# Decode attention with a gated feed-forward on one core: maxima over partitions on GpSimd, w1 and w3 multiplied on VectorE, two programs moved to block boundaries

## The chip, the cores and the metric

The kernel runs on one core of a Trainium2 chip. The metric is the device time of one execution in microseconds; lower is better. All data are float32.

## What is computed

One token x (512 values) goes through grouped-query attention over a cache of 32768 positions (32 query heads, 8 key and value heads, 128 values a head) and through a gated feed-forward (1792 hidden values); a sigmoid gate mixes the two.

```python
def _A_ref(x, k_cache, v_cache, wq, wo):
    q = (x @ wq).reshape(B, Sq, Hq, Dh).transpose(0, 2, 1, 3)
    k = jnp.repeat(k_cache, rep, axis=1)
    v = jnp.repeat(v_cache, rep, axis=1)
    scores = jnp.einsum("bhqd,bhkd->bhqk", q, k) * (Dh ** -0.5)
    p = softmax(scores, axis=-1)
    o = jnp.einsum("bhqk,bhkd->bhqd", p, v)
    return o.transpose(0, 2, 1, 3).reshape(B, Sq, Hq * Dh) @ wo

def _B_ref(x, w1, w3, w2):
    return (silu(x @ w1) * (x @ w3)) @ w2

g = sigmoid((x * gate_w).sum(-1, keepdims=True))
out = g * _A_ref(...) + (1 - g) * _B_ref(...)
```

The caches are 134 MB each and the weights 28 MB in all; every byte is read once.

## The kernel before, in words

**Buffers and loads.** Two large buffers in SBUF, big_a and big_b, have two halves each; the names A0, A1, B0, B1 stand for the halves. All loads go through SyncE's queue in the order of the source: `load` (issued at line 191) and `load_credit` (line 413, values). An issue waits until the readers of its half are done, and everything behind it in the queue waits too. The order is wq (A0, A1), w1 (B0), w3 (B1), then tiles of 4 MB of keys into one half each, then keys and values by turns.

**Start.** GpSimd fills the constants (lines 215 to 225): `ident` with a select at line 218, `ones`, and zeros for padding. Line 255 turns x into columns `xp`. Line 270 multiplies wq. In the block `ff` (line 307) TensorE multiplies w1 and w3 by x, 16 products of 448 columns for each matrix, into the PSUM banks `pf[2]` and `pf[3]`. Lines 313 to 320 make the gated hidden row and turn it.

**Loop.** There are 16 key tiles `t` (4 groups `w` of 4). For each half of a tile VectorE transposes the keys in four parts of 2048 columns (line 355, `kt`), and TensorE multiplies them with a window of the queries (line 344). After both halves ScalarE copies the scores out (line 361). After each fourth tile TensorE turns the scores (`turn`, line 371) into `turned`, four PSUM banks. TensorE's part is a loop in its program (lines from 658 on); the other engines' parts are written out. The values follow the keys by four tiles: `softmax(w)` runs once for each group, behind the key transposes of a tile on VectorE; `weights` (line 418) and `values_all` (line 430) then multiply a tile of values in big_b, and only after that SyncE may load the next values there.

**Softmax.** Line 381 takes the maximum over the free dimension into `mt` (128 x 8). The maximum over the partitions is taken on VectorE: a transpose of 32 x 32 blocks (383), four reductions (385) and one over their results (387), four copies that spread it (390), a transpose back (392). The result `top` is subtracted in place (393), ScalarE takes the exponentials (398), VectorE their sums (403). The queue of VectorE is in order.

**End.** The last group's softmax stands outside the loop, behind `own(11)`. It is followed by the division (`norm`), the placing of heads, and the products with wo (`mix`, line 527), each of which frees `wo_t` for the next load of wo. The last values, wo and w2 arrive while those run; lines 617 to 641 are the last products, the copy of the result, and its write, for which GpSimd waits at the very end.

Of the kernel before, what the change touches and what calls it, by code (L numbers as in the profile page):

```python
# [1 line left out]

# [7 lines left out]
ALU = mybir.AluOpType  # L10
AX = mybir.AxisListType
PE = mybir.EngineType.PE

P = 128
# [102 lines left out]
def kernel(  # L117
# [16 lines left out]
    F = w1.shape[1]  # L134
    HQ = wq.shape[1] // DH
    REP = HQ // HKV
    NC = D // P
# [12 lines left out]
    FJ = F // 4  # L150
# [17 lines left out]
    win = sbuf("win", NP, 4, 48)  # L168
    winc = sbuf("winc", 4, 32)
    probs = sbuf("probs", 2, 65 * 16)  # L170
    prob = [probs[:, u, :] for u in range(2)]
    pv = sbuf("pv", 33 * 16)
# [5 lines left out]
    otp = sbuf("otp", 8, 32)  # L178
    htp = sbuf("htp", FR, 32)
    turned = nc.alloc_psum_tensor("turned", [P, 2048], F32)[:]  # L180
    pf = [turned[:, 512 * f:512 * f + 512] for f in range(4)]
# [12 lines left out]
    def region(b, z):  # L194
        return big[b][:, z * R:(z + 1) * R]

    wqd = wq.rearrange("(p c) n -> p (c n)", c=NC)
    for z in range(2):
        load(region(0, z), wqd[:, z * R:(z + 1) * R], [f"A{z}"])
        if z == 0:  # L200
            load(rows[0][0:1, :], x.rearrange("a b n -> (a b) n"), ["row0"])
            pr.add("ACT", lambda: nc.scalar.dma_start(rows[1][0:1, :], gate_w.rearrange("(o n) -> o n", o=1)),
                   writes=["row1"], inc="gate", by=16)
# [1 line left out]
        load(region(1, z)[:, 0:NC * F], t.rearrange("(p c) f -> p (c f)", c=NC), [f"B{z}"])  # L205


    ident, ones, fold = sbuf("ident", P), sbuf("ones", P), sbuf("fold", 32)
    own_b, own_q, own_k, own_x = sbuf("own_b", 4), sbuf("own_q", 4), sbuf("own_k", 8), sbuf("own_x", 16)
    spot, mask, xp = sbuf("spot", 8, 16), sbuf("mask", 8), sbuf("xp", NC, 32)  # L210
    gate, sums, recip, on = sbuf("gate", 2), sbuf("sums", 32), sbuf("recip", 32), sbuf("on", 32)
    mt, mtt = sbuf("mt", 32), sbuf("mtt", 32)
    quads, high, wide_t, top = sbuf("quads", 4), sbuf("high", 1), sbuf("wide_t", 32), sbuf("top", 32)
    G = nc.gpsimd
    pool(lambda: G.memset(acc, 0.0), writes=["acc"])
    pool(lambda: G.memset(xp, 0.0), writes=["xp0"])
# [2 lines left out]
        out=ident, in_=ident, compare_op=ALU.not_equal, fill=1.0, base=0, pattern=[[-1, P]], channel_multiplier=1,  # L219
    ), reads=["ident0"], writes=["ident"])  # L220
    pool(lambda: G.memset(ones, 1.0), writes=["ones"])
    for n, t in (
        ("win0", win), ("otp", otp), ("mt", mt), ("pvpad", pv[:, 512:528]), ("pad0", prob[0][:, 1024:1040]), ("pad1", prob[1][:, 1024:1040])
    ):
        pool(lambda t=t: G.memset(t, 0.0), writes=[n])

    for src, dst, view, axes in (
# [11 lines left out]
            reads=[src], writes=[dst])  # L239
# [24 lines left out]
    for c in range(NC):  # L264
# [19 lines left out]
        reads=["gate0"], writes=["gate1"])  # L284
# [4 lines left out]
    for b in range(2):  # L289
        qt = kt[b][:, 0:512]  # L290
        dve(lambda b=b, qt=qt: V.transpose(qt, rows[b]), reads=[f"row{b}"], writes=[f"kt{b}"])
        for j in range(4):
            w, u = divmod(4 * b + j, 2)
            src = qt[32 * j:32 * j + 32, :].rearrange("p (q c x) -> p x c q", q=4, c=4)[:, 0]
            for e in range(2):
                r, o = 2 * u + e, 16 + 8 * e + 4 * u
                dst = win[32 * r:32 * r + 32, w, :, o:o + 4]
                act(lambda d=dst, s=src: A.copy(d, s), reads=[f"kt{b}", "win0"], writes=[("win", w, r)])


    for z in range(2):
        def ff(z=z):
            t = region(1, z)
            for c in range(NC):
                for j in range(4):
                    o = c * F + FJ * j
                    ins = T.matmul(  # L307
                        pf[2 + z][32 * j:32 * j + 32, 0:FJ], xp[:, c, :], t[:, o:o + FJ],
                        start=(c == 0), stop=(c == NC - 1),
                    )  # L310
            return ins
        pe(ff, reads=[f"B{z}", "xp"], writes=[f"f{2 + z}"])
    act(lambda: A.activation(silu[:, 0:FJ], pf[2][:, 0:FJ], AF.Sigmoid), reads=["f2"], writes=["silu0"])
    dve(lambda: V.tensor_mul(silu[:, 0:FJ], silu[:, 0:FJ], pf[2][:, 0:FJ]), reads=["f2", "silu0"], writes=["tmp0"])

# [62 lines left out]
    def softmax(w):  # L378
        banks = [f"f{f}" for f in range(4)]

        dve(lambda: V.tensor_reduce(mt[:, 0:8], turned.rearrange("p (n q) -> p q n", q=8), axis=AX.X, op=ALU.max),  # L381
            reads=banks, writes=["mt"])
        dve(lambda: V.transpose(mtt, mt), reads=["mt"], writes=["mtt"])
        for k in range(4):
            dve(lambda k=k: V.tensor_reduce(quads[0:32, k:k + 1], mtt[32 * k:32 * k + 32, :], axis=AX.X, op=ALU.max),  # L385
                reads=["mtt"], writes=[("quads", k)])
        dve(lambda: V.tensor_reduce(high[0:32, :], quads[0:32, :], axis=AX.X, op=ALU.max),
            reads=[("quads", k) for k in range(4)], writes=["high"])
        for k in range(4):
            dve(lambda k=k: V.tensor_copy(wide_t[32 * k:32 * k + 32, :], high[0:32, :].to_broadcast([32, 32])),  # L390
                reads=["high"], writes=[("wide_t", k)])
        dve(lambda: V.transpose(top, wide_t), reads=[("wide_t", k) for k in range(4)], writes=["top"])
        dve(lambda: V.tensor_tensor(  # L393
            turned.rearrange("p (n q) -> p n q", q=8), turned.rearrange("p (n q) -> p n q", q=8),
            top[:, 0:8].unsqueeze(1).to_broadcast([P, 256, 8]), op=ALU.subtract,
        ), reads=["top"], writes=banks)
        for u in range(2):
            act(lambda u=u: A.activation(  # L398
                prob[u][:, 0:1024].rearrange("p (y n q) -> p n y q", y=16, q=4),
                turned.rearrange("p (n y u q) -> p n y u q", n=16, y=16, u=2)[:, :, :, u],  # L400
                AF.Exp, scale=SCALE,
            ), reads=banks, writes=[("prob", u)])
        dve(lambda: V.tensor_reduce(  # L403
            sums[:, 8 * w:8 * w + 8].rearrange("p (u q) -> p u q", u=2),
            probs[:, :, 0:1024].rearrange("p u (n q) -> p u q n", q=4), axis=AX.X, op=ALU.add,
        ), reads=[("prob", u) for u in range(2)], writes=[("sums", w)])
# [46 lines left out]
    for t in range(NH):  # L453
        v = t - LAG
        scores(t, 0, first)
        second = window(t, 1)
        if v >= 1:
            own(v - 1)
            if v % 4:
                vals[v] = (vals[v], weights(v))  # L460
        scores(t, 1, second)
        scores_out(t)
        if t + 1 < NH:
            load_keys(t + 1)
            first = window(t + 1, 0)

        if v >= 0 and v % 4 == 0:
            softmax(v // 4)
            vals[v] = (vals[v], weights(v))
        if v >= 0:  # L470
            values_loop(*vals.pop(v))
        if v + 1 >= 0 and t + 1 < NH:
            vals[v + 1] = load_values(v + 1)
        if t % 4 == 3:
            turn()
# [89 lines left out]
    load(big[1], vd[6, 1], ["B0", "B1"])  # L565
    own(11)
    softmax(3)
    norm(range(4))
    heads(range(6))
# [65 lines left out]
    for a, b in parts[2:]:  # L635
        ff_down([(htp[:, k, :], w2t[:, k, :], k == 8, k == FR - 1) for k in range(a, b)], reads=["htp", ("w2", a)])
        if a == 8:
# [4 lines left out]
           reads=["res"], inc="out", by=16)  # L642


    for e in ("SP", "ACT", "DVE", "POOL"):
        pr.emit(e)
    ops = pr.ops["PE"]
# [60 lines left out]
```

## Time and profile before

| what | value |
|---|---|
| median of three runs | 696.18 us (696.12 to 696.57) |
| the profiled execution's own time | 695.86 us |
| its span in the profile | 694.0 us |
| busy: PE, DVE, ACT, POOL | 402.1, 376.2, 45.3, 2.6 us |
| bytes read from HBM | 296.23 MB |

The profile is one execution. The own time is what the clock of the device gave for it; the span runs from the first to the last instruction that was recorded, so about 1.9 us lie around it. PE is TensorE, DVE VectorE, ACT ScalarE, POOL GpSimd, SP SyncE; a q behind the name means the engine's sequencer, which issues DMAs. In the timeline a row has its start, its duration, engine, line, operation, output and input, and in brackets how long the engine was idle before and what released it.

### The profile page before, as it was taken

The numbers are of one execution on the slowest core, as the hardware profiler recorded it, in microseconds if no ns is written. First come the engines' busy times: TensorE is split into PE (matmuls) and PEld (weight loads), VectorE is DVE, ScalarE is ACT, GpSimd is POOL, SyncE is SP. The second block draws the span as 40 slices with busy tenths as digits, with TensorE's granted clock in tenths as the row PEclk, the third lists the DMA queues.
The fourth block names the chain that finished last, engine by engine and source line by source line (L and its number), as shares of the span: only waits on it lengthen the run. The fifth ranks groups of instructions, "written<-read, shape, count | busy, mean of one in ns | idle before, by whom it ended". The sixth has DMA issues, their size and how long they took to land. (4 is left out here: it accounts for less than half of the span.)

```text
span 694.0 us, 5676 instructions
## 1 busy us (share of the span) xinstructions
PE 402.1 (58%) x2400; PEld 92.6 (13%) x2400; DVE 376.2 (54%) x263; ACT 45.3 (7%) x90; POOL 2.6 (0%) x15
## 2 busy tenths in 40 slices
PE   3636566647556554746667644538456555376756
PEld 1100001101010110201010101201010101131112
DVE  1029999885719081686619091786529090654121
ACT  0200000020100000010100000020100000100000
POOL 1000000000000000000000000000000000000000
PEclk9966877877887796867665898977876776777679
DMA  9999999999999999999999999999999999999996
GB/s 391 421 425 444 431 425 433 467 399 427 451 419 431 444 448 404 450 423 427 465 406 448 416 442 419 442 431 450 427 423 434 419 472 399 447 425 424 427 422 285
DMA packets 9380, 296.34 MB, mean 427 GB/s; under 512 B 1046, under 2 KB 1050, under 8 KB 1436
## 3 DMA queue, kind: packets, MB, share of 16 engines
q1 hardware_dynamic: 9362, 296.23, 99.2%
q8 instruction: 5, 0.08, 0.0%
q14 instruction: 3, 0.02, 0.0%
q10 hardware_dynamic: 10, 0.00, 0.0%
HBM read 296.23 MB, written 0.00 MB: 427 GB/s over the span
## 5 line engine op out<-in xcount | busy, mean ns | idle before, releaser
L355 DVE STREAM_TRANSPOSE kt<-big_a 128x2048 f32<-128x2048 f32 x112 | 250.2, 2287 | 182.3 <-DMA big_a<-in_A_k_cache_dram 180.8
L344 PE MATMUL ps<-kt,winc 128*32 128x512 f32 x1024 | 186.1, 807 | 132.7 <-PEq L658 132.7
L430 PE MATMUL ps<-big_b,pv 128*32 128x512 f32 x768 | 110.2, 738 | 74.0 <-PEq L658 74.0
L344 PEld LDWEIGHTS ps<-kt,winc 128*32 128x32 f32 x1024 | 26.5, 122 | 287.0 <-issue 287.0
L430 PEld LDWEIGHTS ps<-big_b,pv 128*32 128x32 f32 x768 | 30.3, 132 | 153.7 <-issue 153.7
L355 DVE STREAM_TRANSPOSE kt<-big_b 128x2048 f32<-128x2048 f32 x16 | 35.7, 2287 | 3.2 <-DMA big_b<-in_A_k_cache_dram 3.2
L527 DVE SCALAR_TENSOR_TENSOR acc<-wo_t,own_rows,acc 128x512 f32<-128x512 f32 x24 | 18.0, 752 | 28.2 <-DMA wo_t<-in_A_wo_dram 27.4
L244 PE MATMUL ps<-acc 128*128 128x512 f32 x34 | 20.5, 687 | 21.8 <-PEq L658 20.3
L338 ACT COPY winc<-win 128x128 f32<-128x128 f32 x32 | 9.8, 307 | 341.9 <-PE ps L344 341.9
L540 PE MATMUL ps<-big_b,probs 128*32 128x512 f32 x128 | 19.4, 767 | 14.2 <-DMA big_b<-in_A_v_cache_dram 14.2
L361 ACT COPY sb<-ps 128x512 f32<-128x512 f32 x16 | 17.0, 1063 | 151.3 <-PE ps L344 151.3
L540 PE MATMUL ps<-big_a,probs 128*32 128x512 f32 x128 | 20.7, 811 | 5.1 <-DMA big_a<-in_A_v_cache_dram 5.1
L403 DVE TENSOR_REDUCE sums<-probs 128x8 f32<-128x2048 f32 x4 | 15.3, 3822 | 8.0 <-ACT probs L398 8.0
L442 DVE TENSOR_TENSOR tmp<-ps,own_b 128x512 f32<-128x512 f32 x12 | 7.9, 655 | 20.1 <-PE ps L430 20.1
L307 PE MATMUL turned<-big_b,xp 128*32 128x448 f32 x64 | 9.2, 734 | 9.6 <-DMA big_b<-in_B_w_dram 9.6
L270 PE MATMUL turned<-big_a,xp 128*32 128x512 f32 x64 | 11.7, 902 | 2.7 <-DMA big_a<-in_A_wq_dram 2.4
L446 DVE TENSOR_REDUCE red<-tmp 128x128 f32<-128x1024 f32 x6 | 11.5, 1915 | 0.2
L244 PEld LDWEIGHTS ps<-acc 128*128 128x128 f32 x34 | 5.4, 201 | 39.1 <-issue 37.6
L398 ACT ACTIVATE probs<-turned 128x1024 f32<-128x1024 f32 x8 | 7.8, 1021 | 38.5 <-DVE turned L393 38.5
L393 DVE TENSOR_TENSOR turned<-turned,top 128x2048 f32<-128x2048 f32 x4 | 9.2, 2300 | 0.1
L381 DVE TENSOR_REDUCE mt<-turned 128x8 f32<-128x2048 f32 x4 | 9.0, 2260 | 0.0
L549 DVE TENSOR_SCALAR red<-ps,own_b 128x128 f32<-128x128 f32 x2 | 0.7, 348 | 15.3 <-PE ps L540 15.3
(80 smaller groups left out, 95.7 us busy)
## 6 DMA issues: line engine op xcount, KB each, us to landing
big_a<-in_A_k_cache_dram SPq DMA_DIRECT2D x28, 4096.0 KB, 28.3
big_b<-in_A_k_cache_dram SPq DMA_DIRECT2D x4, 4096.0 KB, 30.7
big_a<-in_A_v_cache_dram SPq DMA_DIRECT2D x4, 4096.0 KB, 27.7
big_a<-in_A_wq_dram SPq DMA_DIRECT2D x2, 4096.0 KB, 16.4
wo_t<-in_A_wo_dram SPq DMA_DIRECT2D x4, 2048.0 KB, 18.0
big_b<-in_B_w_dram SPq DMA_DIRECT2D x2, 3584.0 KB, 33.7
big_b<-in_A_v_cache_dram SPq DMA_DIRECT2D x1, 4096.0 KB, 27.3
big_b<-in_A_v_cache_dram SPq DMA_DIRECT2D x2, 2048.0 KB, 34.0
```

What stands on the lines that cost most here:

```text
L244: return T.matmul(ps_s, acc[:, 0:P], acc, start=True, stop=False, skip_group_check=True)
L270: ins = T.matmul(pf[b][32 * j:32 * j + 32, :], xp[:, c, :], t[:, o:o + REP * DH], start=(c == 0), stop=(c == NC - 1),)
L307: ins = T.matmul(pf[2 + z][32 * j:32 * j + 32, 0:FJ], xp[:, c, :], t[:, o:o + FJ], start=(c == 0), stop=(c == NC - 1),)
L338: lambda: A.copy(winc, win[:, t // 4, :, 16 - 16 * z:48 - 16 * z]),
L344: ins = T.matmul(ps_s[32 * g:32 * g + 32, :], winc[:, c, :], kt[c % 2][:, 512 * g:512 * g + 512], start=False, stop=False, skip_group_chec ...
L355: k = dve(lambda c=c, d=dst: V.transpose(d, kin[:, c]), reads=[key], writes=[f"kt{c % 2}"], credit="keys")
L361: lambda: A.copy(sb[:, :, :, t % 4], ps_s.rearrange("p (n i) -> p n i", i=32)),
L403: dve(lambda: V.tensor_reduce(sums[:, 8 * w:8 * w + 8].rearrange("p (u q) -> p u q", u=2), probs[:, :, 0:1024].rearrange("p u (n q) -> p u ...
L430: ins = T.matmul(ps_o[32 * t:32 * t + 32, :], pv[:, o:o + 32], big[1][:, n * P:(n + 4) * P], start=((z, g) == (0, 0)), stop=((z, g) == (1, ...
L446: dve(lambda: V.tensor_reduce(red[h], tmp.rearrange("p e b d -> p d (e b)"), axis=AX.X, op=ALU.add), reads=["tmp0", "tmp1"], writes=[("red ...
L527: dve(lambda k=k: V.scalar_tensor_tensor(acc, wo_t[:, k, :], own_rows[:, w, k:k + 1], acc, op0=ALU.mult, op1=ALU.add,), reads=["wo", ("own ...
L540: ins = T.matmul(ps_o[32 * t:32 * t + 32, :], prob[u][:, o:o + 32], vt[:, n * P:(n + 4) * P], start=((e, z, g) == (0, 0, 0)), stop=((e, z, ...
```

## The change

Three edits. In `softmax` the eleven VectorE instructions of lines 383 to 392 are replaced by one GpSimd instruction, `partition_all_reduce` with max over 128 partitions, from `mt` (now 128 x 8, and no longer filled with zeros at the start) to `top`. In the start VectorE multiplies w1 and w3 in place: for each matrix one multiply by the column `xp` of the first 1792 columns and three multiply-adds for the other three, all into the first 1792 columns; TensorE then only sums over the partitions with `lead` (a matrix whose first column is ones), 4 products of 448 columns for each matrix instead of 16. Before the programs of ScalarE and VectorE stands an alignment to 128 instructions.

```diff
-    ident, ones, fold = sbuf("ident", P), sbuf("ones", P), sbuf("fold", 32)
+    ident, ones, lead, fold = sbuf("ident", P), sbuf("ones", P), sbuf("lead", 32), sbuf("fold", 32)
...
+    pool(lambda: G.memset(lead, 0.0), writes=["lead0"])
+    pool(lambda: G.memset(lead[:, 0:1], 1.0), reads=["lead0"], writes=["lead"])
...
     for z in range(2):
-        def ff(z=z):
-            t = region(1, z)
-            for c in range(NC):
-                for j in range(4):
-                    o = c * F + FJ * j
-                    ins = T.matmul(
-                        pf[2 + z][32 * j:32 * j + 32, 0:FJ], xp[:, c, :], t[:, o:o + FJ],
-                        start=(c == 0), stop=(c == NC - 1),
-                    )
+        h = region(1, z)[:, 0:NC * F].rearrange("p (c f) -> p c f", c=NC)
+        for c in range(NC):
+            xc = xp[:, c, 0:1]
+            if c == 0:
+                go = lambda h=h, xc=xc: V.tensor_scalar(h[:, 0, :], h[:, 0, :], xc, None, op0=ALU.mult)
+            else:
+                go = lambda h=h, xc=xc, c=c: V.scalar_tensor_tensor(
+                    h[:, 0, :], h[:, c, :], xc, h[:, 0, :], op0=ALU.mult, op1=ALU.add,
+                )
+            dve(go, reads=[f"B{z}", "xp"], writes=[f"B{z}"])
+
+        def ff(z=z, h=h):
+            for j in range(4):
+                ins = T.matmul(
+                    pf[2 + z][32 * j:32 * j + 32, 0:FJ], lead, h[:, 0, FJ * j:FJ * j + FJ], start=True, stop=True,
+                )
             return ins
-        pe(ff, reads=[f"B{z}", "xp"], writes=[f"f{2 + z}"])
+        pe(ff, reads=[f"B{z}", "lead"], writes=[f"f{2 + z}"])
...
-        dve(lambda: V.transpose(mtt, mt), reads=["mt"], writes=["mtt"])
...
-        dve(lambda: V.transpose(top, wide_t), reads=[("wide_t", k) for k in range(4)], writes=["top"])
+        pool(lambda: G.partition_all_reduce(top, mt, P, bass_isa.ReduceOp.max), reads=["mt"], writes=["top"])
...
+    A.addr_align(128, offset=0, max_nops=0)
+    V.addr_align(128, offset=0, max_nops=0)
     for e in ("SP", "ACT", "DVE", "POOL"):
         pr.emit(e)
```

More of the change, by code (lines that the diff above doesn't have):

```diff
@@ L3 @@
 import concourse.bass as bass
+import concourse.bass_isa as bass_isa
 import concourse.tile as tile
@@ L211 @@
     gate, sums, recip, on = sbuf("gate", 2), sbuf("sums", 32), sbuf("recip", 32), sbuf("on", 32)
-    mt, mtt = sbuf("mt", 32), sbuf("mtt", 32)
-    quads, high, wide_t, top = sbuf("quads", 4), sbuf("high", 1), sbuf("wide_t", 32), sbuf("top", 32)
+    mt, top = sbuf("mt", 8), sbuf("top", 8)
     G = nc.gpsimd
@@ L221 @@
     pool(lambda: G.memset(ones, 1.0), writes=["ones"])
+    pool(lambda: G.memset(lead, 0.0), writes=["lead0"])
+    pool(lambda: G.memset(lead[:, 0:1], 1.0), reads=["lead0"], writes=["lead"])
     for n, t in (
-        ("win0", win), ("otp", otp), ("mt", mt), ("pvpad", pv[:, 512:528]), ("pad0", prob[0][:, 1024:1040]), ("pad1", prob[1][:, 1024:1040])
+        ("win0", win), ("otp", otp), ("pvpad", pv[:, 512:528]), ("pad0", prob[0][:, 1024:1040]), ("pad1", prob[1][:, 1024:1040])
     ):
@@ L379, in softmax @@
         banks = [f"f{f}" for f in range(4)]
-        dve(lambda: V.tensor_reduce(mt[:, 0:8], turned.rearrange("p (n q) -> p q n", q=8), axis=AX.X, op=ALU.max),
+        dve(lambda: V.tensor_reduce(mt, turned.rearrange("p (n q) -> p q n", q=8), axis=AX.X, op=ALU.max),
             reads=banks, writes=["mt"])
[L383 to L391, printed above, removed]
-        dve(lambda: V.transpose(top, wide_t), reads=[("wide_t", k) for k in range(4)], writes=["top"])
+        pool(lambda: G.partition_all_reduce(top, mt, P, bass_isa.ReduceOp.max), reads=["mt"], writes=["top"])
         dve(lambda: V.tensor_tensor(
             turned.rearrange("p (n q) -> p n q", q=8), turned.rearrange("p (n q) -> p n q", q=8),
-            top[:, 0:8].unsqueeze(1).to_broadcast([P, 256, 8]), op=ALU.subtract,
+            top.unsqueeze(1).to_broadcast([P, 256, 8]), op=ALU.subtract,
         ), reads=["top"], writes=banks)
```

## The prediction

> **What bounds the kernel now.** I read the page's header and its DMA part first, then the timeline of the end, then SyncE's issues against the landings that follow them.
>
> ```profile
> span 694.0 us, 5676 instructions
> DMA  9999999999999999999999999999999999999996
> DMA packets 9380, 296.34 MB, mean 427 GB/s; under 512 B 1046, under 2 KB 1050, under 8 KB 1436
> q1 hardware_dynamic: 9362, 296.23, 99.2%
> 686.00:690.00 4.00, 2.61 (x56) 1.26 (x56) 0.69 (x1) 0.00 (x0) 0.00 (x0) 1.00 0.67 265
> 690.00:694.00 4.00, 0.78 (x24) 0.25 (x12) 0.29 (x1) 0.00 (x0) 0.00 (x0) 1.00 0.00 1
> 689.71 1.06 PE L631 MATMUL turned<-big_a,htp 128*32 128x128 f32 x24 [0.16 <-DMA big_a<-in_B_w_dram]
> 690.85 0.29 DVE L640 COPY res<-turned 128x128 f32<-128x128 f32 x1 [2.45 <-PE turned L631]
> 691.17 0.60 ACTq L641 DMA_DIRECT2D out_dram<-res  x1
> ```
>
> The first four lines: the 16 DMA engines are full in every slice but the last, and one queue accounts for 99.2% of their span. The two window rows (columns: PE, PEld, DVE, ACT, POOL busy; granted clock; DMA share; GB/s) place the end of that stream between 686 and 690 us. The last three rows are all that follows it: the last product at 689.71, the copy, the write of the output at 691.17, and 694.0 - 691.17 = 2.8 us until the span ends. So the time is the stream (about 689 us, 296 MB) plus a tail of about 5 us. An edit on VectorE, GpSimd or TensorE can cost time in three ways only: it holds a buffer so long that the DMA engines run dry, it lengthens the tail, or it delays the first issues. For the same reason no edit here can gain anything in the stream: the bytes stay.
>
> **Cover in the stream.** What a late issue may cost is read from what is still landing when SyncE issues.
>
> ```profile
> 167.41 0.33 SPq L413 DMA_DIRECT2D big_b<-in_A_v_cache_dram  x1
> 177.09 8.95 DVE L355 STREAM_TRANSPOSE kt<-big_a 128x2048 f32<-128x2048 f32 x4 [0.25 <-DMA big_a<-in_A_k_cache_dram]
> 478.00 0.33 SPq L413 DMA_DIRECT2D big_b<-in_A_v_cache_dram  x1
> 487.48 4.50 DVE L355 STREAM_TRANSPOSE kt<-big_a 128x2048 f32<-128x2048 f32 x2 [0.28 <-DMA big_a<-in_A_k_cache_dram]
> 621.33 0.33 SPq L191 DMA_DIRECT2D wo_t<-in_A_wo_dram  x1
> 628.02 9.93 PE L540 MATMUL ps<-big_b,probs 128*32 128x512 f32 x64 [5.53 <-DMA big_b<-in_A_v_cache_dram]
> ```
>
> The pairs are an issue that waits behind a softmax, and the landing of the load queued just ahead of it. Behind the first softmax the values are issued at 167.41 while keys land until 177.09: 9.7 us of queued work. Behind the third it is 487.48 - 478.00 = 9.5 us. Behind the last softmax the projection is issued at 621.33 while values land until 628.02: 6.7 us. An issue must also travel; the output's way from issue to the end of the span is 2.8 us, with the closing of the program in it, so I take 2 us. Free delay is then 7.5 us for each softmax in the loop and 4.7 us for the last one.
>
> **Maxima on GpSimd, four times.**
>
> ```profile
> 147.49 2.25 DVE L381 TENSOR_REDUCE mt<-turned 128x8 f32<-128x2048 f32 x1
> 149.78 0.21 DVE L383 STREAM_TRANSPOSE mtt<-mt 128x32 f32<-128x32 f32 x1
> 152.09 2.30 DVE L393 TENSOR_TENSOR turned<-turned,top 128x2048 f32<-128x2048 f32 x1
> 598.98 0.21 DVE L383 STREAM_TRANSPOSE mtt<-mt 128x32 f32<-128x32 f32 x1
> 601.29 2.30 DVE L393 TENSOR_TENSOR turned<-turned,top 128x2048 f32<-128x2048 f32 x1
> 0.96 0.53 POOL L215 MEMSET acc<- 128x512 f32 x1 [0.52 <-ACTq L154]
> L218 POOL TENSOR_SCALAR_AFFINE_SELECT ident<-ident x1: 293/293/293, 2.0 to 2.0; 128x128 f32<-128x128 f32 x1
> 167.31 8.96 DVE L355 STREAM_TRANSPOSE kt<-big_a 128x2048 f32<-128x2048 f32 x4 [7.10 <-DMA big_a<-in_A_k_cache_dram]
> ```
>
> Removed are the eleven small VectorE instructions from the first transpose to the last: 152.09 - 149.78 = 601.29 - 598.98 = 2.3 us. Added is one GpSimd instruction on 128x8, with VectorE waiting before its subtraction. Queued behind that wait on VectorE are the subtraction, the sums and the key transposes of the next tile; ScalarE's exponentials wait for the subtraction, the value products for them, and SyncE's next value load for these. The trace has no reduction over partitions on GpSimd. Below, one instruction of its kind costs 0.29 us (the select). Above, seven halvings of the partitions and seven steps back are 14 instructions: 14 x 0.29 = 4.1 us, or 14 x 0.53 = 7.4 us at the price of the memset of acc. I take 4.1, as the select, which also tells partitions apart, is the nearest row in kind. The softmax then ends 4.1 - 2.3 = 1.8 us later (from 2.0 earlier to 5.1 later). In the loop that is under 7.5 us, and VectorE had waited 7.1 us for the next keys (167.31 row). For the last softmax 1.8 is under 4.7; only the upper end, 5.1, would show, with 0.4 us. Sum: 0, bounds 0 to +0.4. A gain is excluded, as an earlier issue only lengthens a queue that is never empty.
>
> The Trainium skill, GPSIMD Engine Reference, section 3.2, gives 247,699 ns for a partition-axis tensor_reduce of [128, 2048]. By that, worked in proportion to 8 columns, one maximum would be an estimated 1.0 us, and the sum would be 0 as well; no run here shows it yet.
>
> **w1 and w3 on VectorE.**
>
> ```profile
> 31.13 3.21 PE L307 MATMUL turned<-big_b,xp 128*32 128x448 f32 x32 [2.86 <-DMA big_b<-in_B_w_dram]
> 34.40 13.09 SPq L191 DMA_DIRECT2D big_b<-in_A_k_cache_dram  x2
> 41.12 5.97 PE L307 MATMUL turned<-big_b,xp 128*32 128x448 f32 x32 [6.78 <-DMA big_b<-in_B_w_dram]
> 47.26 0.98 DVE L316 SCALAR_TENSOR_TENSOR row<-tmp,gate,turned 128x448 f32<-128x448 f32 x1 [11.65 <-PE turned L307]
> 48.27 0.65 DVE L320 STREAM_TRANSPOSE htp<-row 128x448 f32<-128x448 f32 x1
> 50.81 8.96 DVE L355 STREAM_TRANSPOSE kt<-big_a 128x2048 f32<-128x2048 f32 x4 [1.89 <-DMA big_a<-in_A_k_cache_dram]
> 60.59 8.95 DVE L355 STREAM_TRANSPOSE kt<-big_a 128x2048 f32<-128x2048 f32 x4 [0.83 <-DMA big_a<-in_A_k_cache_dram]
> 70.24 8.91 DVE L355 STREAM_TRANSPOSE kt<-big_b 128x2048 f32<-128x2048 f32 x4 [0.69 <-DMA big_b<-in_A_k_cache_dram]
> 80.03 8.96 DVE L355 STREAM_TRANSPOSE kt<-big_b 128x2048 f32<-128x2048 f32 x4 [0.88 <-DMA big_b<-in_A_k_cache_dram]
> L527 DVE SCALAR_TENSOR_TENSOR acc<-wo_t,own_rows,acc 128x512 f32<-128x512 f32 x24 | 18.0, 752 | 28.2 <-DMA wo_t<-in_A_wo_dram 27.4
> ```
>
> For each matrix VectorE gets one multiply and three multiply-adds on 1792 columns, and TensorE keeps 4 of 16 products. From the 2048-column subtraction: 2.30 x 1792/2048 = 2.0 us each, 8.0 us for four; from the 512-column multiply-add: 0.752 x 3.5 = 2.6, 10.5 us for four. I take 8.0, since a row near in length has its fixed part in the right proportion. TensorE's quarter is 3.21/4 = 0.8 to 5.97/4 = 1.5 us. w1 lands at 31.13: VectorE until 39.1 (41.6), the half of big_b free at 40 to 43 instead of 34.40. Still queued then are w3 (41.12) and keys until 60.59, 17 us at least. w3 lands at 41.12: VectorE until 49.1 (52.1), its half free at 50 to 54 instead of at 34.40 + 13.09 = 47.5, with keys queued until 60.59, 6 us at the worst end and the other key load behind it. Then L316 and L320, 1.6 us: the first key transposes begin at about 51.6 (55.2 at the upper end) instead of 50.81. Their buffer is released up to 4.4 us late, when loads until 70.24 and 80.03 are queued. Each half brings 9.8 us of DMA (70.24 to 80.03) for 8.96 of VectorE, so the lag also dies away. Sum: 0. The cover is those queued keys; without them the edit would cost at least the 5.6 us by which w1's half comes free later.
>
> **Boundaries of programs.** One skip before VectorE's and ScalarE's first instruction. VectorE's first work waits for GpSimd's ident, and the code of both engines' later work stays in order. Sum: 0; if a block's end moved into the tail, a fetch there would cost about the output's way, 2.8 us; nothing in the trace makes that likely.
>
> **What the program of GpSimd carries.** This is the term that decides.
>
> ```profile
> L218 POOLq MODIFY_POOL_CONFIG  x2: 11/11/11, 1.9 to 2.0; - x2
> L218 POOLq MOVE  x1: 35/35/35, 1.8 to 1.8; - x1
> 3.42 0.16 POOL L225 MEMSET probs<- 128x16 f32 x2
> 1.36 0.33 SPq L191 DMA_DIRECT2D row<-in_A_x_dram  x1
> 12.97 0.61 PE L255 MATMUL ps<-ident,row 1*128 1x1 f32 x4 [9.35 <-DMA row<-in_A_x_dram]
> ```
>
> Ahead of the only special GpSimd instruction of the kernel before stand two configuration instructions that nobody wrote in the source; they take 11 ns each, and the select follows at 2.00. So GpSimd's functions come in sets, and the set for the select is already there at the start of every execution. If the new maximum belongs to another set, that set is loaded once ahead of it, and the first one has to come back once per execution: at the end of the program, or at the select of the next one. A load ahead of the first maximum has from 3.6 us, where the setup ends, to 149.78 if it stands before the wait. Behind the wait, it adds to the first softmax. At the select it delays ident, and TensorE waits for x until 12.97 anyway. At the end, behind the wait for the output, nothing covers it.
>
> A real load isn't in the trace. Below: 0.2 us (the pair at 1.9 until the select). Above: 11.6 us, a small transfer under full traffic from issue (1.36) to use (12.97). At the end the queues are empty, so the nearest row is the output's 2.8 us; emptying one set and fetching another are two such ways, 5.6 us, which I take as an estimate.
>
> The Trainium skill, GPSIMD Engine Reference, section 2.1, says that the first call to a freshly loaded kernel pays an IRAM load of approximately 6 us (5.95) with no visible profile instruction. By that figure the term would be 6.0 instead of 5.6; this trace holds no such load, so it neither agrees nor disagrees.
>
> **Sum.** 0 (maxima) + 0 (w1, w3) + 0 (boundaries) + 5.6 (the set put back in the tail) on the profiled span: 694.0 + 5.6 = 699.6. The profiled execution's own time was 695.86, 1.9 us more than its span, and the median of the runs is 696.18; with the same 5.6 they become 701.5 and 701.8. I forecast 701.8.
>
> **Rivals.**
> 1. Nothing shows. The set comes back at the next select or ahead of the output's wait, or the maximum needs no other set. For it: the stream's cover above, and the wait for x until 12.97 at the start. Against it: a program that ends with a foreign set would find the select's pair slow, and in this trace the pair is fast. Time: 696.2, 695.6 to 697.2 with run to run spread.
> 2. The load stands behind the first softmax's wait, under full traffic. Price: up to 11.6 + 1.8 = 13.4 us of delay against 7.5 free, 5.9 us, if the end is free: 702.1; it decides from 5.7 us of load on (5.7 + 1.8 = 7.5). For it: the MOVE of L218 stands ahead of the pair, so a pair can lie behind a wait.
> 3. The maximum itself takes over 7 us (4.7 free + 2.3 removed). At 10 us the last softmax costs 3 us: 699.2; the loop's three stay covered up to 9.8 us. Against it: the GpSimd rows above are 0.29 us for 128 columns and 0.53 for 512, and this one has 8.
> 4. Faster: only the tail could shrink, and no edit touches it except by the place of a block's end. 694 to 694.7.
>
> **How the numbers follow.** Forecast 0.50, rival 1 0.35, rival 2 0.06, rival 3 0.05, rival 4 0.04. What a measurement of this kernel can tell from no change is about 0.2%, 1.4 us. Slower: 0.50 + 0.06 + 0.05 = 0.61; two in a hundred of these would stay within the bound, as a load of under 1.4 us is possible, so 0.59, within 0.37, faster 0.04. The forecast's own range, from a load of half the estimate to one and a half, is 699.0 to 704.6. The whole range reaches down to rival 1's middle, 695.8, and up to 704.6: it leaves out rival 4, the lower edge of rival 1 and the high end of the load.
>
> **What would show it.** In the profile after: configuration instructions on GpSimd a second and a third time, the last behind the output's write, with the span longer by 5 to 7 us while the last product still starts near 689.7. The DMA line stays at 9 in every slice until the end. The maxima: GpSimd instructions of 0.3 to 7 us, with VectorE's idle time before L393's line equal to them. At the start the first key transposes begin at 51 to 55 us. Wrong would be: the last product later than 691 (then the stream had gaps, and the slice where DMA falls names the step), a span that ends within 3.5 us of the output's issue (rival 1), or a gap in the DMA share after 177 us (rival 2) or 628 us (rival 3).

## The result and the profile after

The changed kernel takes 698.16 us (median of ten runs, 697.51 to 698.65) against 696.22 us for the kernel before (ten runs, 695.94 to 696.57): +1.94 us, ratio 1.0027 (95% interval 1.0017 to 1.0037). The profiled execution's own time is 698.65 us, the longest of its ten; its span is 696.8 us, so again 1.9 us lie around it. Slower was forecast, and the time lies in the range, but the forecast was +5.6 us, and that term is not where it was placed.

The page of the kernel after, the lines that answer to those of before:

```profile
span 696.8 us, 5551 instructions
DMA  9999999999999999999999999999999999999995
DMA packets 9380, 296.33 MB, mean 425 GB/s; under 512 B 1046, under 2 KB 1050, under 8 KB 1436
q1 hardware_dynamic: 9362, 296.23, 98.8%
q8 instruction: 4, 0.07, 0.0%
q14 instruction: 4, 0.03, 0.0%
```

The two queues of program code on the page of the kernel before:

```profile
q8 instruction: 5, 0.08, 0.0%
q14 instruction: 3, 0.02, 0.0%
```

The bytes are the same and the DMA line is full until the last slice. The rows of q8 and q14 say how many pieces of program code were fetched by these queues, 16 KB each in q8 and 8 KB each in q14. The sum is 8 in both kernels; the row of q14 becomes important below.

The timeline of the end, kernel after:

```profile
692.58 1.06 PE L632 MATMUL turned<-big_a,htp 128*32 128x128 f32 x24 [0.18 <-DMA big_a<-in_B_w_dram]
693.71 0.29 DVE L641 COPY res<-turned 128x128 f32<-128x128 f32 x1 [2.38 <-PE turned L632]
694.03 0.60 ACTq L642 DMA_DIRECT2D out_dram<-res  x1
```

The tail is as before: from the last product to the output's issue 1.45 us (before 1.46), and 2.8 us from there to the span's end (before 2.8). All of the lost time lies ahead of the last product, which waits for its weights until 692.58 instead of 689.71. (These are 2.87 us in the profiled execution, the longest of its ten; between the medians it is 1.94.) Windows of 2 us around that point (columns as in the prediction: PE, PEld, DVE, ACT, POOL busy; granted clock; DMA share; GB/s), first the kernel before, then after:

```profile
688.00:690.00 2.00, 1.37 (x44) 1.10 (x48) 0.40 (x1) 0.00 (x0) 0.00 (x0) 1.00 0.33 131
690.00:692.00 2.00, 0.78 (x24) 0.25 (x12) 0.29 (x1) 0.00 (x0) 0.00 (x0) 1.00 0.00 0
```

```profile
688.00:690.00 2.00, 1.92 (x18) 0.32 (x16) 0.00 (x0) 0.00 (x0) 0.00 (x0) 1.00 0.44 177
690.00:692.00 2.00, 1.25 (x32) 0.68 (x28) 0.69 (x1) 0.00 (x0) 0.00 (x0) 1.00 0.07 27
692.00:694.00 2.00, 1.46 (x40) 0.67 (x32) 0.29 (x1) 0.00 (x0) 0.00 (x0) 1.00 0.02 8
```

The share counts 16 engines. Before, all the engines are done ahead of 690. After, a share of 0.07 is 0.07 x 16 = 1.1 engines over two whole microseconds: from about 690 one DMA engine works on alone, and the last product waits for it. The records of the single packets show the same: half a microsecond before the last packet ends, six packets are still under way in the kernel before, and in the kernel after there is one at a time for the last 2.5 us. Its last sixteen are eight of the 128 packets of 4 KB and eight of the 128 packets of 2 KB with which the loads end, a sixteenth of each. The time is not the mean of the stream; it is the latest of 16 engines.

The timeline of the start, kernel after, and the group of L393:

```profile
1.39 2.93 ACTq L203 DMA_DIRECT2D row<-in_gate_w_dram  x1
L218 POOLq MODIFY_POOL_CONFIG  x2: 11/11/11, 2.0 to 2.0; - x2
13.12 0.28 POOL L218 TENSOR_SCALAR_AFFINE_SELECT ident<-ident 128x128 f32<-128x128 f32 x1 [11.37 <-issue]
13.46 0.63 PE L257 MATMUL ps<-ident,row 1*128 1x1 f32 x4 [9.86 <-POOL ident L218]
L393 POOLq MODIFY_POOL_CONFIG  x2: 11/11/11, 15.0 to 15.1; - x2
```

The same two configuration instructions stand ahead of the select, but the select now starts at 13.12 instead of 2.00. The reading, which runs e4 to e7 bear out below: its set is really loaded, and the exchange stands at the start, where the last execution left the other set behind. The second pair, for the maximum, stands at 15.0, ahead of the maximum's wait, where nothing waits for it until 151 us.

The maxima (group and timeline), kernel after:

```profile
L393 POOL PARTITION_ALL_REDUCE top<-mt x4: 365/366/397, 151.4 to 600.5; - x4
598.16 2.28 DVE L391 TENSOR_REDUCE mt<-turned 128x8 f32<-128x2048 f32 x1
600.93 2.30 DVE L394 TENSOR_TENSOR turned<-turned,top 128x2048 f32<-128x2048 f32 x1 [0.49 <-POOL top L393]
```

One maximum takes 0.37 to 0.40 us. VectorE stands still for 600.93 - 600.44 = 0.49 us, where eleven instructions had taken 2.3: each softmax ends 1.8 us earlier, not later.

w1 and w3 on VectorE (timeline), kernel after:

```profile
33.80 1.11 DVE L309 TENSOR_SCALAR big_b<-big_b,xp 128x1792 f32<-128x1792 f32 x1
34.95 6.33 DVE L311 SCALAR_TENSOR_TENSOR big_b<-big_b,xp 128x1792 f32<-128x1792 f32 x3
43.11 8.76 SPq L192 DMA_DIRECT2D big_b<-in_A_k_cache_dram  x2
53.20 8.91 DVE L365 STREAM_TRANSPOSE kt<-big_a 128x2048 f32<-128x2048 f32 x4
```

The four operations of w1 take from 33.80 to 41.28, 7.5 us (forecast 8.0); its half comes free at 43.11 (forecast 40 to 43); the first key transposes begin at 53.20 (forecast 51 to 55). They begin 2.7 us later than the 31.13 from which the forecast counted; run e2 shows what that does to the comparison.

### The profile page after: what moved, and what is told of

The parts are those of the page before. It is cut to its first block, busy times and chain, and to the rows that moved or that the text cites. A ratio compares the mean times of both kernels' runs of the same rounds, so it can differ in the third digit from the quotient of the medians.

```text
span 696.8 us, 5551 instructions
## 1 busy us (share of the span) xinstructions
PE 403.5 (58%) x2352; PEld 91.2 (13%) x2352; DVE 382.4 (55%) x227; ACT 45.3 (7%) x90; POOL 4.2 (1%) x20
## 5 line engine op out<-in xcount | busy, mean ns | idle before, releaser
L354 PE MATMUL ps<-kt,winc 128*32 128x512 f32 x1024 | 190.4, 824 | 126.4 <-PEq L662 126.4
L431 PE MATMUL ps<-big_b,pv 128*32 128x512 f32 x768 | 111.7, 746 | 70.6 <-PEq L662 70.6
L318 PE MATMUL turned<-big_b,lead 128*32 128x448 f32 x16 | 3.4, 955 | 16.2 <-DVE big_b L311 16.2
L311 DVE SCALAR_TENSOR_TENSOR big_b<-big_b,xp 128x1792 f32<-128x1792 f32 x6 | 12.5, 2084 | 0.2
```

What stands on the lines that cost most here:

```text
L311: go = lambda h=h, xc=xc, c=c: V.scalar_tensor_tensor(h[:, 0, :], h[:, c, :], xc, h[:, 0, :], op0=ALU.mult, op1=ALU.add,)
L354: ins = T.matmul(ps_s[32 * g:32 * g + 32, :], winc[:, c, :], kt[c % 2][:, 512 * g:512 * g + 512], start=False, stop=False, skip_group_chec ...
L431: ins = T.matmul(ps_o[32 * t:32 * t + 32, :], pv[:, o:o + 32], big[1][:, n * P:(n + 4) * P], start=((z, g) == (0, 0)), stop=((z, g) == (1, ...
```

## The experiments

Each run has its kernel before on the same chip; "+1.42" is the difference of the two medians in us, with the ratio and its interval. A number of these kernels carry two explicit loads of GpSimd's function sets, called set 1 (the maximum's) and set 0 (the select's); such a load does no other work. The letters in the expectations are the theories' names there; the text after each says what became of them.

**1 to 3: each part alone.**

e1_maxima: the kernel after without the alignment and with w1 and w3 on TensorE as before.

> The maxima on GpSimd alone, with w1, w3 and the start of the programs as before. Theory A (GpSimd loads two sets of functions in every execution, in the first 26 us, and these loads hold back some of the 16 DMA engines): slower than before by 1.2 to 2.4 us, select at about 13 us, last product at 691 to 693 us. Theory B (the multiplies of w1 and w3 on VectorE hold big_b too long): no change, within 0.5 us. Theory C (fetches of code behind the alignment): no change.

697.54 against 696.12: +1.42, 1.0020 (1.0011 to 1.0029). Its select starts at 13.61.

e2_w1w3: only w1 and w3 on VectorE.

> w1 and w3 on VectorE alone. Theory A: no change, within 0.5 us, with the first key transposes 1 to 2 us later than before. Theory B: slower by 1.2 to 2.4 us. Theory C: no change.

696.25 against 696.12: +0.13, 1.0001 (0.9992 to 1.0010), no difference that can be told. The timeline of this kernel:

```profile
31.30 1.15 DVE L308 TENSOR_SCALAR big_b<-big_b,xp 128x1792 f32<-128x1792 f32 x1 [0.82 <-DMA big_b<-in_B_w_dram]
40.65 8.84 SPq L191 DMA_DIRECT2D big_b<-in_A_k_cache_dram  x2
50.82 8.91 DVE L364 STREAM_TRANSPOSE kt<-big_a 128x2048 f32<-128x2048 f32 x4
```

The half of w1 comes free 40.65 - 34.40 = 6.25 us later than before, at no cost: the cover by queued keys holds. The first key transposes begin at 50.82, as in the kernel before (50.81). So this part alone doesn't move them; the 53.20 of the kernel after comes from its late start.

e3_align: only the two alignments.

```diff
+    A.addr_align(128, offset=0, max_nops=0)
+    V.addr_align(128, offset=0, max_nops=0)
```

> The alignment of the two programs alone. Theory A: no change, within 0.5 us, although ScalarE's first issue takes about 3 us instead of 0.5. Theory B: no change. Theory C: slower by 1.2 to 2.4 us.

697.16 against 696.12: +1.04, 1.0015 (1.0006 to 1.0024). A part that was priced at nothing costs half of the total. The three parts give 1.42 + 0.13 + 1.04 = 2.59, more than the 1.94 of the whole: they don't simply add.

**4: loads alone.** The kernel before, with set 1 loaded behind the setup, so that sets are exchanged as in the kernel after and no maximum runs on GpSimd.

```diff
+    pool(lambda: G.load_library(library_config.all_libraries[1]), by=0)
```

> The kernel before with one more instruction on GpSimd behind its setup: it asks for the second set of functions, which nothing then uses. Theory A: two real loads in every execution, select at about 13 us, slower by 1.2 to 2.4 us, like the maxima alone. Theories B and C, or a cost of the maxima themselves: no change, within 0.5 us.

697.46 against 696.12: +1.34, 1.0021 (1.0012 to 1.0030). The timeline of this kernel:

```profile
13.29 0.28 POOL L219 TENSOR_SCALAR_AFFINE_SELECT ident<-ident 128x128 f32<-128x128 f32 x1 [11.53 <-issue]
```

The exchange alone gives what the maxima gave (+1.42). The maximum itself costs nothing.

**5 and 6: the kernel after with a single set.** Set 1 is loaded ahead of the select, which runs from it too, so that nothing is exchanged any more; e6 also leaves out both alignments.

```diff
     pool(lambda: G.memset(acc, 0.0), writes=["acc"])
+    pool(lambda: G.load_library(library_config.all_libraries[1]), by=0)
```

> The changed kernel with one instruction more at its start, which names for the select the set that the maximum needs too, so that after the first execution no set is exchanged. Theory A (the two loads per execution hold back DMA engines; the alignment adds its own cost of about 1.0 us): select at about 2 us again, 1.0 us over before (697.0 to 697.4). Theory A2 (the alignment's cost and the loads' don't add; they fall on different DMA engines and the later one counts): the same. Rival D (the time comes from GpSimd's maximum or from its waits): no better than the change, 1.9 us over before.

> The same without the alignment: maxima on GpSimd and w1, w3 on VectorE, one set of functions. Theory A: the time of before within 0.4 us, select at about 2 us. Rival D: 1.3 us or more over before.

e5: 697.12 against 696.09, +1.03, 1.0014 (1.0005 to 1.0023). e6: 696.06 against 696.09, 0.9999 (0.9990 to 1.0008). The select in e5's timeline:

```profile
2.09 0.29 POOL L220 TENSOR_SCALAR_AFFINE_SELECT ident<-ident 128x128 f32<-128x128 f32 x1 [0.15 <-POOL ident L219]
```

Without the exchange the alignment's +1.0 is left, without both nothing is left, and the maxima and w1, w3 are still as in the kernel after. This settles the split. It also is the best version that was found, and it equals the kernel before; none beats it.

**7: is it ident, or the load?** In e4 the load delays ident and with it TensorE's start. Here the kernel before loads set 1 and then set 0 behind the setup, so that ident is early.

```diff
+    for i in (1, 0):
+        pool(lambda i=i: G.load_library(library_config.all_libraries[i]), by=0)
```

> The kernel before with both loads behind GpSimd's setup: the second set is asked for and then the first again; nothing uses the second, ident is early (2.3 us). Theory A (what counts is the loads' own traffic on the DMA engines): 1.0 to 1.7 us over before, as with the loads around the select. Rival E (what counts is that ident and with it x and the first products come late): no change, within 0.4 us.

697.61 against 696.09: +1.52, 1.0020 (1.0011 to 1.0029), with the select at 2.25. The late ident is not the cause; the loads beside the first weights are. They hold back the transfers themselves: TensorE's first products wait for x here, not for ident, and start at 13.62 instead of 12.97. The row of those products, and the configuration instructions of the two loads (first and last start in us):

```profile
13.62 0.60 PE L258 MATMUL ps<-ident,row 1*128 1x1 f32 x4 [10.01 <-DMA row<-in_A_x_dram]
L228 POOLq MODIFY_POOL_CONFIG  x4: 7/9/11, 3.8 to 14.1; - x4
```

From the first pair to the second lie 14.1 - 3.8 = 10.3 us: the first load.

**8, 12, 13, 14, 17: where the same two loads stand.** They are tied to a point in the run by a small memset that waits there.

```diff
+        if w == 1:
+            pool(lambda: G.memset(dummy, 0.0), reads=["mt"], writes=["dummy"])
+            for i in (1, 0):
+                pool(lambda i=i: G.load_library(library_config.all_libraries[i]), by=0)
```

e8_loads_mid, behind the second softmax's first reduction:

> The kernel before with the same two loads in the middle of the stream, behind the second softmax's first reduction (about 306 us). Theory A: the loads hold back some DMA engines wherever they fall, and nothing evens this out: 1.0 to 1.7 us over before. Rival E: no change, since the start is untouched. Rival F (the loads matter only at the start, when the queues of all engines are being filled): no change as well.

696.05 against 696.09, 0.9999 (0.9990 to 1.0009). The theory that the loads cost the same wherever they fall is wrong.

e12_loads_keys, behind the turn of the hidden row, under the first keys:

> The kernel before with the two loads of sets at about 49 us, when the first keys arrive, two small steps later than the weights. Theory F (the loads cost time only while the first weights stream, before the order of the queues has settled): no change, as with the loads in the middle. Rival J (they cost time in the whole early part, and only the middle was free): 1.0 to 1.7 us over before.

696.95 against 696.16: +0.79, 1.0014 (1.0005 to 1.0023). So it isn't the first weights alone; the theory that only loads beside them cost is wrong as it was worded.

e13_loads_late, as e8 with w == 3, near the last softmax:

> The kernel before with the two loads at about 599 us, when the last values and wo arrive. Theory F: no change, each load in about 6 us. Rival K (weights and the sets of functions lie where their reads collide in HBM, so loads beside weights cost time): 0.5 us or more over before and loads of 8 us or more.

696.12 against 696.16, 1.0000 (0.9991 to 1.0009). The theory by which loads near the end would cost is wrong too.

e14_loads_midkeys, tied to the second softmax's sums, so that keys stream beside the loads:

> The kernel before with the two loads of sets behind the second softmax's sums (about 316 us), when keys stream in 32 KB packets; at 306 us, where they cost nothing, values streamed in 64 KB packets. Theory N (what streams beside the loads decides): the first load takes 9 us or more, some packets are 0.3 us longer, and some DMA engines stay late; time 0 to 1.7 us over before, as it falls. Theory F (only the early part counts): the first load in about 6 us, no longer packets, no change.

696.04 against 696.11, 0.9999 (0.9990 to 1.0008). What streams beside the loads, keys or values, doesn't decide.

e17_loads_first, as e8 with w == 0:

> The kernel before with the two loads of sets behind the first softmax's first reduction (about 150 us), between 49 us, where they cost 0.8 us, and 306 us, where they were free. Theory F (only the early part counts, the end of it unknown): if the first load takes about 6 us, no change; if it takes 9 us or more, 0.4 to 1.7 us over before. Rival O (a load that is not waited for by anything at the start is always free): no change and about 6 us.

696.17 against 696.12, 1.0002 (0.9993 to 1.0011). Neither expectation fits fully: the load is longer than the later ones, and yet it costs nothing. The configuration rows of e12, e17, e8, e14 and e13, one fence for each kernel:

```profile
L329 POOLq MODIFY_POOL_CONFIG  x4: 7/9/11, 49.2 to 58.9; - x4
```

```profile
L388 POOLq MODIFY_POOL_CONFIG  x4: 7/9/11, 150.5 to 159.1; - x4
```

```profile
L388 POOLq MODIFY_POOL_CONFIG  x4: 5/8/11, 306.2 to 312.2; - x4
```

```profile
L412 POOLq MODIFY_POOL_CONFIG  x4: 7/9/11, 316.7 to 323.1; - x4
```

```profile
L388 POOLq MODIFY_POOL_CONFIG  x4: 5/8/11, 599.2 to 605.7; - x4
```

The first load takes 10.3 us at 4 us into the run, 9.7 at 49, 8.6 at 150, 6.0 at 306, 6.4 at 317 and 6.5 at 599. The two earliest cost 1.5 and 0.8 us of the run; from 150 us on they are free. The records of the packets separate the two kinds. A packet of 32 KB takes 1.22 us as a rule. In e7 seven of them take 0.4 to 1.3 us longer, in two groups that start at 8.6 to 8.9 and 19.0 to 19.9 us, one behind each of the two loads; in e12 seven take 0.3 to 0.7 us longer, at 54.8 to 54.9 and 62.8 to 64.0 us. In e17, e8, e14 and e13 no packet beside the loads is 0.3 us longer, apart from the ones behind a fetch of code, which the kernel before has too. So the price comes together with packets of the stream that take longer, and not with the load's duration. Why packets take longer beside the early loads only is open.

**9 and 10: which alignment.** One line each, ScalarE's and VectorE's.

> The alignment of ScalarE's program alone. Theory H (ScalarE's first issue, the load of gate_w, waits for code that is fetched through the DMA engines at 2 to 4 us, and the engine that carries both is late for the rest of the run): the alignment's whole cost, 0.7 to 1.3 us over before, ScalarE's issue takes about 3 us. Theory I (VectorE's fetch is the one that costs): no change, within 0.4 us.

> The alignment of VectorE's program alone. Theory H: no change, within 0.4 us, ScalarE's issue takes 0.5 us as before. Theory I: 0.7 to 1.3 us over before.

e9: 696.19 against 696.16, 1.0001 (0.9992 to 1.0010). e10: 697.06 against 696.16, +0.90, 1.0015 (1.0006 to 1.0024). ScalarE's first issue in e9's timeline and its code fetches, then the same of e10:

```profile
1.40 2.57 ACTq L202 DMA_DIRECT2D row<-in_gate_w_dram  x1
q14 instruction: 3, 0.02, 0.0%
```

```profile
0.96 0.53 ACTq L202 DMA_DIRECT2D row<-in_gate_w_dram  x1
q14 instruction: 4, 0.03, 0.0%
```

The visible change at the start, ScalarE's issue at 1.40 instead of 0.96, belongs to the alignment that is free. The one that costs shows nothing but a fourth fetch of code. By the packets' start times the fetches of q14 lie at 131, 159 and 454 us in the kernel before, at 2, 131 and 455 in e9, and at 4, 159, 300 and 618 in e10. So the one at 159 is ScalarE's, which the alignment of ScalarE moves to the start, and the other two are VectorE's, which become three. The added one in e10 lasts 0.32 us, from 3.90 to 4.22; a packet of the stream starts where it ends and takes 1.73 us instead of 1.22. On the engine of these two that is 0.32 + 0.51 = 0.83 us, near the 0.90 that the run loses.

**15 and 16: is it one late engine?** If the latest of 16 engines sets the time, 128 KB in eight single rows of 16 KB should cost much more than the same 128 KB spread over 128 rows. Both are loaded behind the first keys into buffers that are free at that time, and nothing reads them.

```diff
+    for i in range(8):
+        load(wo_t[16 * i:16 * i + 1].rearrange("o k e -> o (k e)"), v_cache[0, i, 0:32, :].rearrange("(o s) d -> o (s d)", o=1), [("spare", i)])
```

```diff
+    load(wo_t.rearrange("p k e -> p (k e)")[:, 0:256], v_cache[0, 0, 0:256, :].rearrange("(p s) d -> p (s d)", p=P), ["spare"])
```

> The kernel before with eight loads of one row of 16 KB each (128 KB in all, into a buffer that is not in use yet and is overwritten later) behind the first keys. Theory L (every DMA engine has its fixed share of every load, work that falls on one engine makes it late for the rest of the run, and the latest engine sets the time): 0.6 us over before if the rows fall on eight engines, up to 4.9 us if all fall on one. Rival M (only the sum of the bytes counts, 128 KB of 296 MB at 430 GB/s): 0.3 us over before.

> The same 128 KB as one load of 128 rows of 1 KB, which all engines share. Theories L and M: 0.2 to 0.4 us over before.

e15: 701.85 against 696.11, +5.74, 1.0083 (1.0069 to 1.0096). e16: 696.42 against 696.11, +0.31, 1.0004 (0.9995 to 1.0013). The windows of the end, e15 and then e16:

```profile
690.00:692.00 2.00, 2.00 (x14) 0.46 (x10) 0.00 (x0) 0.00 (x0) 0.00 (x0) 1.00 0.40 159
692.00:694.00 2.00, 1.38 (x12) 0.16 (x8) 0.47 (x1) 0.00 (x0) 0.00 (x0) 1.00 0.12 49
694.00:696.00 2.00, 1.63 (x48) 1.19 (x48) 0.21 (x1) 0.00 (x0) 0.00 (x0) 1.00 0.05 22
```

```profile
688.00:690.00 2.00, 1.18 (x34) 0.74 (x32) 0.69 (x1) 0.00 (x0) 0.00 (x0) 1.00 0.54 213
690.00:692.00 2.00, 1.40 (x38) 0.60 (x28) 0.29 (x1) 0.00 (x0) 0.00 (x0) 1.00 0.02 9
```

Spread, the bytes cost too little to be told from nothing; unspread they cost 5.7 us, and a share of 0.05 (0.8 engines) is left at 694 to 696, where e16 is long done. The packets' records show why it isn't eight times less: the eight rows are eight packets of 16 KB, one behind the other without a gap from 58.4 to 65.7 us, so one engine got them all. What it gets late there stays: the last packet of the first tile of values ends at 163.0 us instead of 157.1, the last packet of 64 KB at 633.3 instead of 627.5, the last packet of all at 695.6 instead of 689.9, which is 5.9, 5.8 and 5.7 us. e15 also has a fourth fetch of code on its page, at 651 us, whose price was not measured by itself; at the 0.9 to 1.06 us of the early one, between 4.7 and 5.7 of the 5.74 belong to the rows, 0.6 to 0.7 us each.

**18: another place for VectorE's program.** The alignment of e10 with an offset of 64 instead of 0.

```diff
+    V.addr_align(128, offset=64, max_nops=0)
```

> VectorE's program alone, aligned to 64 instructions behind a boundary of 128 instead of to the boundary. Theory L (an engine that carries a code fetch stays about 1 us late, and the cost depends on which DMA engine and which other fetch it meets): the fetches come at other times, and the time is either that of before within 0.4 us or again 0.7 us or more over it; it can't be said which. Rival P (the alignment itself, its skip at the start, costs the time): 0.7 to 1.1 us over before.

697.18 against 696.12: +1.06, 1.0015 (1.0006 to 1.0024). By time alone this doesn't separate the number of fetches from a fixed price of the skip to the boundary. The page has four fetches here too. Among the kernels without exchanges of sets or extra data, those with a fourth fetch (e3, e5, e10, e18) are +0.90 to +1.06, and those with three (e2, e6, e9) are -0.03 to +0.13. The fourth is in all of them a fetch at 3.9 to 4.2 us, also in the kernel after. No kernel has the skip on VectorE without this fetch, so the link is a strong agreement and not a proof; nor do these runs settle whether it costs because it is one more or because it comes so early. (In e9 a fetch at 2 us replaces a later one at no cost, which speaks for the count.) The other queue of code, q8, doesn't follow the time: its row reads 4 in e2, e5, e6 and the kernel after and 5 in the rest.

The windows of e10 and of e4 at the end show the same picture as the kernel after, each with part of its lateness:

```profile
690.00:692.00 2.00, 1.78 (x52) 0.99 (x43) 0.00 (x1) 0.00 (x0) 0.00 (x0) 1.00 0.03 12
```

```profile
690.00:692.00 2.00, 1.79 (x52) 1.26 (x56) 0.04 (x1) 0.00 (x0) 0.00 (x0) 1.00 0.05 18
```

The starts and durations of the packets give the end of the last weights: 689.86 us in the kernel before, 690.11 in e9, 690.07 in e6, 690.04 in e17, 690.35 in e2, 691.01 in e10, 691.03 in e12, 691.22 in e5 and e7, 691.26 in e3, 691.34 in e18, 691.44 in e4, 691.59 in e1, 692.72 in the kernel after. Of these, the kernels that cost nothing end within 0.5 us of the kernel before; each of the others ends over 1.1 us late. In e10 the last nine packets end 0.08 us apart like beads on a string, one engine alone; in the kernel before several end within such a step.

## Why the prediction was right in sign and wrong in size

**What failed: "What the program of GpSimd carries", the term that decided.** It put the set back "in the tail" for 5.6 us. The tail didn't change (2.8 us from the output's issue to the span's end). The set comes back at the select of the next execution, which the prediction named as one of two ways and priced at nothing: "At the select it delays ident, and TensorE waits for x until 12.97 anyway." For ident the cover was too short by little (x goes into columns at 13.46 instead of 12.97, and the copy to `xp` stands at 14.84 instead of 13.61, behind the reductions of ident in VectorE's queue), and it was beside the point, since e7 costs the same with ident early. The reason given against it, that "in this trace the pair is fast", was no evidence: the kernel before uses one set and never has to exchange. In the kernel after the pair takes the same 11 ns, and it is the select behind it that waits. Measured: 1.3 to 1.5 us alone (e4, e1, e7).

**What was mis-sized: "Boundaries of programs", 0.** Measured +1.04 for both (e3), +0.90 for VectorE's alone (e10), nothing for ScalarE's (e9). The argument looked at the instructions' order and at a block's end in the tail, and not at the code fetches that go through the same DMA engines as the data; the page of the kernel before has them, as a queue of 3 packets.

**The step under both: the stream as one queue.** "An edit on VectorE, GpSimd or TensorE can cost time in three ways only: it holds a buffer so long that the DMA engines run dry, it lengthens the tail, or it delays the first issues." There is a fourth: it makes one of the DMA engines late. Lateness of one isn't evened out by the others: in e15 it is 5.9 us at 157 us and 5.7 at the end, and in the kernel after the last engine does its sixteenth of the last loads while the others are idle. By this reading 1.42 and 1.04 need not add: where two delays fall on different engines the larger counts, on the same one the sum. 1.94 lies between 1.42 and 2.46. On which engine a load of a set or a fetch falls isn't in the packet records, so this stays inferred from the single engine at the end.

**Right: the maxima at 0.** e5 and e6 show it. The cost of one was too high, 4.1 us against 0.37 to 0.40, near the lower bound of 0.29; 14 steps at the select's price don't fit into it. The Trainium skill, GPSIMD Engine Reference, section 3.2, in proportion to 8 columns had given an estimated 1.0 us; the measurement is less than half of that. The gain of 1.8 us in each softmax brings nothing, as the prediction said of any earlier issue.

**Right: w1 and w3 at 0**, with 7.5 us against 8.0. That the release at 43.11 and the key transposes at 53.20 lie close to 40 to 43 and inside 51 to 55 is luck: the multiplications began at 33.80 and not at 31.13. In e2, where they begin at 31.30, the release at 40.65 fits, and the transposes at 50.82 lie ahead of the forecast 51.6, since the work on w3 begins at 39.81 instead of 41.12. Neither delay had a price, as argued.

**The load's duration.** The Trainium skill, GPSIMD Engine Reference, section 2.1, has a first-call load of approximately 6 us with no visible profile instruction. From 306 us on the runs agree (6.0 to 6.5 us), and no instruction of the profile has this duration; earlier in the stream they measured 8.6 to 10.3, and the select's wait of 11.4 us in the kernel after includes such a load. Only the pair of configuration instructions ahead of it is visible here, 11 ns each in the kernel after. The duration wasn't the price in either case: 10.3 us of load cost 1.5, and 8.6 us cost nothing.

**What the rivals said.** Rival 1 (nothing shows) had the mechanism right, the exchange at the next select, and the price wrong. Rivals 2 and 3 are refuted by the second pair at 15.0 ahead of the wait and by 0.4 us for a maximum. The announced sign "the last product later than 691 (then the stream had gaps, and the slice where DMA falls names the step)" came in its first half: the last product started at 692.58, with no slice below 9 before the last. A lateness of one engine in sixteen doesn't show in tenths. A second announced sign came too, that of rival 1: the span ends 2.8 us after the output's issue, within 3.5. (The lower end of the range, 695.8, is called rival 1's middle there; by its own line the middle is 696.2.)

**Open.** Why packets of the stream take 0.3 to 1.3 us longer beside loads at 4 and 49 us, and not beside loads at 150 us and later. Whether VectorE's added fetch costs by its early place or as one more. And which engine carries which fetch.

## What to carry to other kernels

When the stream bounds a kernel, ask which of the 16 DMA engines finishes last, and look at the DMA share of the last few microseconds in windows of 2 us: a share near 1/16 that lasts is one late engine, and small extra work on it, a row loaded by itself or a piece of code, is not hidden by the full stream (here 0.6 to 0.7 us a row, 0.9 to 1.06 for the fetch). Before a second kind of GpSimd function is added, ask what the next execution finds loaded; if one set holds both functions, load that one at the start. That the order of the instructions stays doesn't make it free to move where a program begins: compare the counts of the instruction queues on the page.

## What was not expected of the hardware

One engine's lateness stays for 600 us: eight single rows behind the first keys go through one engine and cost 5.74 us at the end, the same bytes over 128 rows 0.31. A move of VectorE's program to a boundary of 128 instructions, or to the middle between two, brings one more 8 KB fetch of code, at 4 us, and 0.9 to 1.1 us. The same load of a GpSimd set takes 10.3 us at 4 us into the run and 6.0 to 6.5 us from 306 us on.
